# Linear attention and a SiLU layer on one core: moving batch 1's softmax steps, W2's first rows and batch 3's loads

## The chip, the core and the metric

The kernel runs on one core of a Trainium2 chip. The core has TensorE (PE, matrix products into PSUM), VectorE (DVE), ScalarE (ACT), GpSimd (POOL) and SyncE (SP), each with its own queue of instructions that it works through in order, and 16 DMA engines that all of them share. The time is that of the device for one execution, in microseconds (us); the figure of a kernel is the median of its runs.

## What is computed

Eight batches, eight heads, 576 positions, 64 columns a head. Attention without the square matrix: q is softmaxed over its 64 columns, k over the positions, and both meet through a 64 x 64 matrix. The result, 4608 rows of 512, goes through a layer with a SiLU.

```python
q_s = softmax(q, axis=-1); k_s = softmax(k, axis=2)
kv  = einsum('bhsd,bhse->bhde', k_s, v)
x   = einsum('bhsd,bhde->bhse', q_s, kv)   # -> x: (4608, 512)
h   = x @ w_in                             # w_in: (512, 2048)
out = (h * sigmoid(h)) @ w_out             # w_out: (2048, 512)
```

Inputs and output are float32; the products run in fp16 and bf16.

## The kernel before

The work is cut into nine chunks of 512 rows of x (`TCH`); the attention is done by batch (576 rows), so that chunk t needs batches up to t. Chunk 0 is special: its first layer is done over all 576 rows of batch 0 (`wide`, 16 blocks of 128 columns of w_in, line 258), so the first 64 columns of chunk 1 (counted along the rows of x) are already there and are copied from GTS[0] to GTS[1]. From chunk 1 on, the two layers are done in the form of Strassen and Winograd: seven products instead of eight, with sums and differences of blocks made on VectorE ahead of them. Their names are WS (`ws_op`, differences of w_in, line 319), XS (`xs_op`, of x, line 329), S (`s_op`, of the SiLU's result GT, line 442) and T (`t_op`, of W2, line 452; T3 is written over a quarter of W2). `group` (line 368) does products of the first layer, `prod` (line 468) of the second; `mm2_plain` (line 405) is chunk 0's second layer, one block of W2's rows at a time, `mm1` (line 276) half of chunk 1's first. `group_snap` copies a group's partial sums from PSUM to a tile h, `group_add` (line 346) adds another to it.

The attention of a batch b has these steps. `load` brings q, k and v in halves `cc` (four heads each) into two buffers per name. `exp_q` (line 108) makes eq; its sums over the 64 columns come from VectorE alone (`qsum`, lines 148 and 150), or, for batch 1, from `qsum_pair` and `qsum_end`: GpSimd adds the halves of the 64 columns twice (lines 126 and 129), and VectorE reduces the 16 that are left (line 136) and inverts them. `qnorm` (line 157) multiplies eq in place. Then eq is transposed, by TensorE (`tr`, line 175, with `trcopy` out of PSUM) for batches 0 and 1 and by a DMA (`q_transpose`, line 167) later. `exp_k` (line 113) makes ek, `vcast` (line 91 or 89) puts v into vaug as bf16, `kv` (line 189) multiplies them, `kvcopy` (lines 200 and 202) divides, and `xt` (line 228) makes the columns of x for a chunk in tiles XT.

The order is written out by hand. `units` is a list of pieces of TensorE's work, and `plan(u, f)` puts f ahead of unit u; `begin[t]` (b1 for chunk 1) is the unit at which a chunk starts. In the order in which this list is walked, each engine gets its instructions, and each works them off in that order. Units 0 to 15 are the blocks of `wide`; from b1 come nine units of `mm2_plain`, then `mm2_plain` and `group` in turn, then eight of `mm1`; `full(t)` lays out chunks 2 to 6. Within a unit the plans are taken in the order in which they stand.

```python
for u, f in enumerate(units):
    for g in at.get(u, ()):
        g()
    f()
```

Loads come from two queues. Before chunk 1 is done they are issued by GpSimd (w_in, w_out with a change of type from float32 to fp16, and q, k, v of batches 1 and 2), later by SyncE, which also stores the output. The tiles of W2 are loaded four blocks of rows at a time (`load_w2`). A load waits for its buffer's last reader; in SyncE's queue everything behind it waits with it.

Of the kernel before, what the change touches and what calls it, by code (L numbers as in the profile page):

```python
# [17 lines left out]
def kernel(  # L18
# [9 lines left out]
    nc = tc.nc  # L28
    B, H, S, D = q.shape
# [3 lines left out]
    J = S // P  # L33
# [4 lines left out]
    TCH = 512  # L38
# [23 lines left out]
    GTS = [glob.tile([128, NFB, S], FP16, name="GT0"), glob.tile([128, NFB, TCH], FP16, name="GT1")]  # L62
# [24 lines left out]
    def copy(eng, o, i):  # L87
        if eng is nc.scalar:
            eng.copy(out=o, in_=i)  # L89
        else:  # L90
            eng.tensor_copy(o, i)  # L91

    def load(b, name, src, cc, eng):
        t = ld.tile([128, 2, J * D], FP32, name=name)
        st[b][name, cc] = t
        x = src[b].rearrange("(g r) (p j) d -> g (r p) (j d)", r=2, j=J)
        eng.dma_start(out=t, in_=x.rearrange("g x y -> x g y")[:, 2 * cc:2 * cc + 2, :])

    def jgd(b, name, cc):
        return st[b][name, cc].rearrange("p g (j d) -> p j g d", d=D)  # L100

    def half(t, cc):
        return t[:, :, cc * 128:(cc + 1) * 128].rearrange("p j (g d) -> p j g d", d=D)

    def exp_q(b, cc, g0=0, g1=2):
        if "eq" not in st[b]:
            st[b]["eq"] = ap.tile([128, J, NG * D], BF16, name="eq")
        nc.scalar.activation(  # L108
            out=half(st[b]["eq"], cc)[:, :, g0:g1], in_=jgd(b, "qt", cc)[:, :, g0:g1], func=ACT.Exp
        )  # L110

    def exp_k(b, cc):
        nc.scalar.activation(out=half(ek, cc), in_=jgd(b, "kt", cc), func=ACT.Exp)  # L113
# [6 lines left out]
    def qsum_pair(b, cc):  # L120
        e = half(st[b]["eq"], cc)
        t1 = mp.tile([128, 2 * TCH], FP32, name="h0", bufs=1)[:, 0:J * D]
        t1 = t1.rearrange("p (j g d) -> p j g d", g=2, d=D // 2)
        t2 = mp.tile([128, 2 * TCH], FP32, name=f"h{cc + 1}", bufs=1)[:, 0:J * D // 2]
        t2 = t2.rearrange("p (j g d) -> p j g d", g=2, d=D // 4)
        nc.gpsimd.tensor_tensor(
            out=t1, in0=e[:, :, :, 0:D // 2], in1=e[:, :, :, D // 2:D], op=ALU.add
        )
        nc.gpsimd.tensor_tensor(
            out=t2, in0=t1[:, :, :, 0:D // 4], in1=t1[:, :, :, D // 4:D // 2], op=ALU.add  # L130
        )
        st[b]["t2", cc] = t2

    def qsum_end(b, cc):
        new_zq(b)
        nc.vector.reduce_sum(out=st[b]["zq"][:, cc], in_=st[b]["t2", cc], axis=AX.X)
        nc.vector.reciprocal(out=st[b]["rzq"][:, cc], in_=st[b]["zq"][:, cc])

    def new_zq(b):
        if "zq" not in st[b]:  # L140
            st[b]["zq"] = ap.tile([128, 2, J, 2], FP32, name="zq", bufs=2)
            st[b]["rzq"] = ap.tile([128, 2, J, 2], FP32, name="rzq", bufs=2)
# [11 lines left out]
    def qnorm(b, cc, eng):  # L154
        e = half(st[b]["eq"], cc)
        r = st[b]["rzq"][:, cc]
        eng.tensor_tensor(  # L157
            out=e, in0=e, in1=r[:, :, :, None].to_broadcast([128, J, 2, D]), op=ALU.mult
        )

    def new_qt(b):
        if "qT" not in st[b]:
            st[b]["qT"] = ap.tile([128, J, 2, 128], BF16, name="qT", bufs=2)
        return st[b]["qT"]
# [7 lines left out]
    def tr(b, cc, j0, j1, bank):  # L172
        t = PS[:, bank, :].bitcast(BF16)
        for j in range(j0, j1):
            nc.tensor.transpose(
                out=t[:, (j - j0) * 128:(j - j0 + 1) * 128],
                in_=st[b]["eq"][:, j, cc * 128:(cc + 1) * 128],
                identity=ident,
            )

    def trcopy(b, cc, j0, j1, bank, eng=nc.vector):
        t = PS[:, bank, :].bitcast(BF16)[:, 0:(j1 - j0) * 128].rearrange("x (j y) -> x j y", y=128)
        copy(eng, new_qt(b)[:, j0:j1, cc, :], t)
# [25 lines left out]
    def kv_both(b):  # L209
        kv(b, 0)  # L210
        kv(b, 1)
        kvcopy(b)
# [25 lines left out]
    def xt(t, cc, eng=nc.scalar):  # L238
        got = pieces(t)
        for b, col, n, dst in got:  # L240
            xt_mm(b, cc, col, n, 6, dst)
        xt_evac(t, cc, 6, got[0][3], TCH, got[0][3], eng)
# [62 lines left out]
    def wa(c, f):  # L305
        return W1[:, 2 * c:2 * c + 2, f * 128:(f + 4) * 128]
# [4 lines left out]
    def ws_op(i, g):  # L311
        w, f0, f1 = WS[g], 4 * g + 8, 4 * g
        in0, in1, op = {
            1: (wa(0, f1), wa(1, f1), ALU.add),
            2: (w[0], wa(0, f0), ALU.subtract),
            3: (wa(0, f0), wa(0, f1), ALU.subtract),
            4: (wa(1, f0), w[1], ALU.subtract),
        }[i]
        nc.vector.tensor_tensor(out=w[i - 1], in0=in0, in1=in1, op=op)
# [30 lines left out]
    def group_silu(t, i, f, n):  # L350
        x = group_bank(t, False) if i is None else four(t, i)
        nc.scalar.activation(out=group_out(t, f, n), in_=x, func=ACT.Silu, scale=1.0 / XS)  # L352
# [46 lines left out]
    def store(t, col, o):  # L399
        for i in range(2):  # L400
            nc.sync.dma_start(out=rows(t, col + i * P), in_=o[i * P:(i + 1) * P, :])
# [11 lines left out]
    def mm2_plain_out(t, m, eng):  # L413
        if m % 2 == 0:
            st[t]["ow"] = mp.tile([128, 2, DM], FP32, name="ow", bufs=3)
        o = st[t]["ow"][:, m % 2]
        if eng is nc.scalar:
            nc.scalar.activation(out=o, in_=PS[:, 2 + m], func=ACT.Copy, scale=OS)
        else:
            nc.vector.tensor_scalar_mul(out=o, in0=PS[:, 2 + m], scalar1=OS)  # L420
        store(t, m * 128, o)
# [22 lines left out]
    def t_op(i, eng, f0=0, f1=HF):  # L444
        o, in0, in1 = {
            1: (T1, B12, B11),
            2: (T2, B22, T1),
            3: (T3, B22, B12),
            4: (T4, B21, T2),
        }[i]  # L450
        f = slice(f0, f1)
        eng.tensor_tensor(out=o[:, f], in0=in0[:, f], in1=in1[:, f], op=ALU.subtract)  # L452
# [97 lines left out]
    def load_w2(f0, f1):  # L550
        nc.gpsimd.dma_start(
            out=W2[:, f0:f1, :],
            in_=w_out[f0 * 128:f1 * 128, :].rearrange("(fc p) o -> p fc o", p=128),
        )
# [10 lines left out]
    load_w1(8, 16, 2, 4)  # L565
    load(1, "qt", q, 0, nc.gpsimd)
    load(1, "qt", q, 1, nc.gpsimd)
    load(1, "kt", k, 0, nc.gpsimd)
    load(1, "kt", k, 1, nc.gpsimd)
    load_w2(0, 4)  # L570
    load_w2(4, 8)
    load(1, "vt", v, 0, nc.gpsimd)
    load(1, "vt", v, 1, nc.gpsimd)
# [39 lines left out]
    def plan(u, f):  # L613
        at.setdefault(u, []).append(f)
# [141 lines left out]
    for i in (1, 2, 6, 5, 7, 4, 3):  # L756
# [3 lines left out]

    b1 = begin[1]

    plan(9, lambda: (load_w2(8, 12), exp_q(1, 0), qsum_pair(1, 0)))
    plan(12, lambda: (exp_q(1, 1, 0, 1), qsum_end(1, 0), qnorm(1, 0, nc.gpsimd)))
    plan(12, lambda: load(2, "qt", q, 0, nc.gpsimd))
    plan(13, lambda: (exp_q(1, 1, 1, 2), qsum_pair(1, 1)))
    plan(14, lambda: load(2, "qt", q, 1, nc.gpsimd))
    plan(b1 + 2, lambda: (exp_k(1, 0), exp_k(1, 1)))
    plan(b1 + 1, lambda: (tr(1, 0, 0, 5, 6), tr(1, 0, 5, J, 7)))
    plan(b1 + 1, lambda: (trcopy(1, 0, 0, 5, 6, nc.scalar), trcopy(1, 0, 5, J, 7)))  # L770
    plan(b1, lambda: (qsum_end(1, 1), qnorm(1, 1, nc.vector)))
    plan(b1, lambda: load_w2(12, 16))
    plan(b1, lambda: nc.gpsimd.tensor_copy(GTS[1][:, :, 0:64], GTS[0][:, :, TCH:S]))
    plan(b1 + 3, lambda: (load(2, "kt", k, 0, nc.gpsimd), load(2, "kt", k, 1, nc.gpsimd)))
    plan(b1 + 6, lambda: (load(2, "vt", v, 0, nc.gpsimd), load(2, "vt", v, 1, nc.gpsimd)))
    plan(b1 + 4, lambda: vcast(1, 0, nc.scalar))
# [17 lines left out]
    plan(b1 + 17, lambda: (vcast(2, 0, nc.gpsimd), vcast(2, 1, nc.gpsimd)))  # L794
    plan(b1 + 22, lambda: (group_silu(1, 2, 4, 1), group_silu(1, 0, 12, 0)))
    plan(b1 + 18, lambda: t_op(1, nc.vector))
    plan(b1 + 23, lambda: mm2_plain_out(0, 0, nc.scalar))
    plan(b1 + 23, lambda: (load(3, "qt", q, 0, nc.sync), load(3, "kt", k, 1, nc.sync)))
    plan(b1 + 23, lambda: mm2_plain_out(0, 1, nc.vector))
    plan(b1 + 24, lambda: group_silu(1, 1, 12, 1))  # L800
    plan(b1 + 24, lambda: (ws_op(1, 0), ws_op(2, 0)))
    plan(b1 + 24, lambda: [load(3, x, y, i, nc.sync) for x, y, i in (
        ("vt", v, 0), ("vt", v, 1), ("kt", k, 0), ("qt", q, 1)
    )])
    plan(b1 + 25, lambda: kv_both(2))
    plan(b1 + 26, lambda: t_op(2, nc.vector))
    plan(b1 + 27, lambda: xt(2, 0, nc.vector))
    plan(b1 + 28, lambda: t_op(4, nc.vector))
    plan(b1 + 29, lambda: xt(2, 1))
# [40 lines left out]
```

The softmax here doesn't subtract the row's maximum and nothing guards it: scores larger than these inputs give would overflow.

## Time and profile before

| | us |
|---|---|
| median of 5 runs | 264.38 (264.09 to 264.59) |
| the profiled execution | 264.04 |
| its span | 262.3 |
| TensorE busy | 252.5 |
| VectorE busy | 208.4 |
| ScalarE busy | 186.6 |
| GpSimd busy | 67.8 |

The span is the part of the execution from the first instruction to the last; the rest lies around it. In a timeline each row is one group of equal instructions in a row: start, time, engine, line, operation, output<-input, shapes, count, and in brackets how long the engine stood idle before it and what released it. L405 is line 405 of the kernel. Ends of matrix products are modelled, so holes in TensorE are better counted from start to start.

### The profile page before, as it was taken

What the parts mean: (1) busy time and instruction counts of PE and PEld (TensorE: products, weight loads), DVE (VectorE), ACT (ScalarE), POOL (GpSimd) and SP (SyncE); (2) the same over time, 40 slices, a digit from 0 to 9 for tenths busy, and PEclk for the clock granted to TensorE, in tenths of its full rate; (3) what the DMA queues carried; (4) which work ended last, traced back from release to release, by engine and by line L of the source; (5) the groups of instructions that cost most, each with busy time, mean ns of one, the idle gap of its engine ahead of it and who ended that gap; (6) DMA issues with size and microseconds to landing.
All of it is one profiled execution on the core that took longest, in us unless ns stands there. A gap on an engine that the chain in (4) does not pass through costs nothing.

```text
span 262.3 us, 6406 instructions
## 1 busy us (share of the span) xinstructions
PE 252.5 (96%) x2732; PEld 203.0 (77%) x2732; DVE 208.4 (79%) x268; ACT 186.6 (71%) x210; POOL 67.8 (26%) x63
## 2 busy tenths in 40 slices
PE   8799999999899999999999999999999999999993
PEld 3457655656788888888888888888888888888882
DVE  2867777799997999799979997999798448855932
ACT  4766874898796699669966997699664757584610
POOL 1653792550450306030603060306000000000004
PEclk9999999999999999999999999999999999999998
DMA  7999999669987487858874889650425002500534
GB/s 246 339 185 324 266 317 331 264 124 308 399 325 165 149 205 276 133 183 202 279 180 139 200 281 119 198 118 2 90 51 112 2 0 48 115 2 1 117 85 120
DMA packets 35452, 45.89 MB, mean 175 GB/s; under 512 B 16208, under 2 KB 19984, under 8 KB 35424
## 3 DMA queue, kind: packets, MB, share of 16 engines
q1 hardware_dynamic: 29488, 33.63, 47.0%
q0 software_dynamic: 5616, 11.60, 17.1%
q8 instruction: 21, 0.34, 0.5%
q10 hardware_dynamic: 320, 0.26, 0.4%
q14 instruction: 7, 0.06, 0.1%
HBM read 36.70 MB, written 9.44 MB: 176 GB/s over the span
## 4 chain that ended last, share of the span: by engine, by line
PE 74%; DVE 9%; DMA 9%; issue 4%; ACT 2%; POOL 1%; POOLq 0%; DVEq 0%; ACTq 0%
PE PS L468 33%; PE PS L368 31%; DMA W<-in_moe_w_out_dram 6%; PE PS L405 4%; DMA W<-in_moe_w_in_dram 3%; PE PS L228 2%; PE PS L189 2%; DVE h L346 2%; DVE S L442 1%; DVE zq L148 1%; DVE T L452 1%; DVE GT L442 1%; ACT ek L113 1%; POOL out_dram L730 1%; PE PS L276 1%
## 5 line engine op out<-in xcount | busy, mean ns | idle before, releaser
L346 DVE TENSOR_TENSOR h<-PS,h 128x1024 f32<-128x1024 f32 (+1 forms) x45 | 54.0, 1199 | 12.0 <-PE PS L368 6.0
L468 PEld LDWEIGHTS <-GT 128*128 128x128 f16 x512 | 49.5, 98 | 6.9 <-issue 1.0
L368 PEld LDWEIGHTS <-WS 128*128 128x128 f16 x480 | 46.7, 98 | 7.1 <-issue 1.0
L468 PE MATMUL PS<-W,GT 128*128 128x256 f16 x384 | 49.1, 273 | 0.0
L368 PE MATMUL PS<-XS,WS 128*128 128x256 f16 (+1 forms) x360 | 46.3, 272 | 0.2
L352 ACT ACTIVATE GT<-h 128x1024 f16<-128x1024 f32 (+1 forms) x45 | 46.1, 1047 | 0.3 <-DVE h L346 0.3
L89 ACT COPY h<-PS 128x1024 f32<-128x1024 f32 (+1 forms) x35 | 35.1, 1003 | 13.2 <-PE PS L368 12.5
L157 POOL TENSOR_TENSOR eq<-eq,rzq 128x1152 bf16<-128x1152 bf16 x13 | 27.5, 2117 | 56.7 <-DVE rzq L152 52.7
L468 PEld LDWEIGHTS <-S 128*128 128x128 f16 x384 | 37.0, 98 | 6.3 <-DVE S L442 1.0
L368 PEld LDWEIGHTS <-W 128*128 128x128 f16 x360 | 34.6, 98 | 4.8 <-issue 0.5
L468 PE MATMUL PS<-T,S 128*128 128x256 f16 x256 | 32.7, 273 | 0.8 <-DVE S L442 0.8
L368 PE MATMUL PS<-XT,W 128*128 128x256 f16 (+1 forms) x240 | 29.5, 272 | 0.1
L352 ACT ACTIVATE GT<-PS 128x1024 f16<-128x1024 f32 (+1 forms) x15 | 15.2, 1016 | 18.9 <-PE PS L368 18.9
L91 POOL CAST vaug<-vt 128x1152 bf16<-128x1152 f32 x12 | 15.4, 1289 | 45.9 <-DMA vt<-in_v_dram 37.5
L730 POOL DMA_DIRECT2D out_dram<-ow x5 | 2.7, 545 | 72.1 <-DVE ow L715 72.1
L108 ACT ACTIVATE eq<-qt 128x1152 bf16<-128x1152 f32 (+1 forms) x17 | 18.8, 1108 | 2.6 <-DMA qt<-in_q_dram 2.6
L113 ACT ACTIVATE ek<-kt 128x1152 bf16<-128x1152 f32 x16 | 18.4, 1155 | 2.8 <-DMA kt<-in_k_dram 2.8
L148 DVE TENSOR_REDUCE zq<-eq 128x18 f32<-128x1152 bf16 x12 | 16.1, 1345 | 3.9 <-ACT eq L108 3.9
L258 PE MATMUL PS<-XT,W 128*128 128x288 f16 x128 | 16.3, 286 | 0.5 <-DVE XT L91 0.2
L468 PE MATMUL PS<-W,S 128*128 128x256 f16 x128 | 16.5, 273 | 0.0
L488 DVE SCALAR_TENSOR_TENSOR ow<-PS,sc 128x512 f32<-128x512 f32 x7 | 4.8, 692 | 14.4 <-ACT sc L484 14.4
L405 PE MATMUL PS<-W,GT 128*128 128x512 f16 x64 | 15.6, 380 | 0.2 <-DMA W<-in_moe_w_out_dram 0.2
(78 smaller groups left out, 344.4 us busy)
## 6 DMA issues: line engine op xcount, KB each, us to landing
out_dram<-ow SPq DMA_DIRECT2D x64, 128.0 KB, 2.4
qt<-in_q_dram SPq DMA_DIRECT2D x12, 576.0 KB, 4.7
kt<-in_k_dram SPq DMA_DIRECT2D x12, 576.0 KB, 5.9
vt<-in_v_dram SPq DMA_DIRECT2D x12, 576.0 KB, 5.4
qt<-in_q_dram POOLq DMA_DIRECT2D x4, 576.0 KB, 11.3
kt<-in_k_dram POOLq DMA_DIRECT2D x4, 576.0 KB, 12.1
vt<-in_v_dram POOLq DMA_DIRECT2D x4, 576.0 KB, 12.0
W<-in_moe_w_out_dram POOLq DMA_DIRECT2D x4, 512.0 KB, 15.1
```

Source lines behind the costliest of these rows:

```text
L89: eng.copy(out=o, in_=i)
L91: eng.tensor_copy(o, i)
L108: nc.scalar.activation(out=half(st[b]["eq"], cc)[:, :, g0:g1], in_=jgd(b, "qt", cc)[:, :, g0:g1], func=ACT.Exp)
L113: nc.scalar.activation(out=half(ek, cc), in_=jgd(b, "kt", cc), func=ACT.Exp)
L148: nc.vector.reduce_sum(out=z, in_=e, axis=AX.X)
L157: eng.tensor_tensor(out=e, in0=e, in1=r[:, :, :, None].to_broadcast([128, J, 2, D]), op=ALU.mult)
L258: nc.tensor.matmul(out=PS[:, 2 * (fb % 3) + n, 0:S // 2], lhsT=W1[:, c, fb * 128:(fb + 1) * 128], rhs=XTS[0][:, c, n * (S // 2):(n + 1) * ...
L346: nc.vector.tensor_tensor(out=four(t, i), in0=group_bank(t, True), in1=four(t, i), op=ALU.add)
L352: nc.scalar.activation(out=group_out(t, f, n), in_=x, func=ACT.Silu, scale=1.0 / XS)
L368: nc.tensor.matmul(out=PS[:, bank + p // 2, (p % 2) * HT:(p % 2) * HT + width(t)], lhsT=a[:, c, p * 128:(p + 1) * 128], rhs=bb[:, c, 0:wid ...
L405: nc.tensor.matmul(out=PS[:, 2 + tb, :], lhsT=GTS[t % 2][:, fc, tb * 128:(tb + 1) * 128], rhs=W2[:, fc, :], start=(fc == 0), stop=(fc == N ...
L468: nc.tensor.matmul(out=PS[:, bank, m * HN:(m + 1) * HN], lhsT=a[:, fc, m * 128:(m + 1) * 128], rhs=bb[:, fc, :], start=(first and fc == 0) ...
```

## The change

Seven moves, all in the order and none in the arithmetic. Batch 1's first exp of q is made in two halves, one ahead of block 9 and one ahead of block 10 of `wide`. The GpSimd sums of both halves of the heads now stand ahead of the GpSimd norm of the first, and the loads of batch 2's q behind it. Batch 1's first transposes and their copies stand two units later, behind its exps of k. The copy of chunk 1's first 64 columns goes from GpSimd to ScalarE and eight units later. W2's first four blocks of rows are loaded ahead of batch 1's k. Batch 3's six loads stand together in SyncE's queue ahead of chunk 0's eight stores, in the order q, k, k, v, v, q (before: q, k, then stores, then v, v, k, q, then stores). WS1 of group 0 is made eleven units earlier, and T2 two.

```diff
     load(1, "qt", q, 1, nc.gpsimd)
+    load_w2(0, 4)
     load(1, "kt", k, 0, nc.gpsimd)
     load(1, "kt", k, 1, nc.gpsimd)
-    load_w2(0, 4)
     load_w2(4, 8)
...
-    plan(9, lambda: (load_w2(8, 12), exp_q(1, 0), qsum_pair(1, 0)))
-    plan(12, lambda: (exp_q(1, 1, 0, 1), qsum_end(1, 0), qnorm(1, 0, nc.gpsimd)))
-    plan(12, lambda: load(2, "qt", q, 0, nc.gpsimd))
-    plan(13, lambda: (exp_q(1, 1, 1, 2), qsum_pair(1, 1)))
-    plan(14, lambda: load(2, "qt", q, 1, nc.gpsimd))
+    plan(9, lambda: (load_w2(8, 12), exp_q(1, 0, 0, 1)))
+    plan(10, lambda: (exp_q(1, 0, 1, 2), qsum_pair(1, 0)))
+    plan(12, lambda: (exp_q(1, 1, 0, 1), qsum_end(1, 0)))
+    plan(13, lambda: (exp_q(1, 1, 1, 2), qsum_pair(1, 1), qnorm(1, 0, nc.gpsimd)))
+    plan(14, lambda: (load(2, "qt", q, 0, nc.gpsimd), load(2, "qt", q, 1, nc.gpsimd)))
     plan(b1 + 2, lambda: (exp_k(1, 0), exp_k(1, 1)))
-    plan(b1 + 1, lambda: (tr(1, 0, 0, 5, 6), tr(1, 0, 5, J, 7)))
-    plan(b1 + 1, lambda: (trcopy(1, 0, 0, 5, 6, nc.scalar), trcopy(1, 0, 5, J, 7)))
+    plan(b1 + 3, lambda: (tr(1, 0, 0, 5, 6), tr(1, 0, 5, J, 7)))
+    plan(b1 + 3, lambda: (trcopy(1, 0, 0, 5, 6, nc.scalar), trcopy(1, 0, 5, J, 7)))
     plan(b1, lambda: (qsum_end(1, 1), qnorm(1, 1, nc.vector)))
     plan(b1, lambda: load_w2(12, 16))
-    plan(b1, lambda: nc.gpsimd.tensor_copy(GTS[1][:, :, 0:64], GTS[0][:, :, TCH:S]))
+    plan(b1 + 8, lambda: nc.scalar.copy(out=GTS[1][:, :, 0:64], in_=GTS[0][:, :, TCH:S]))
...
+    plan(b1 + 23, lambda: [load(3, x, y, i, nc.sync) for x, y, i in (
+        ("qt", q, 0), ("kt", k, 1), ("kt", k, 0), ("vt", v, 0), ("vt", v, 1), ("qt", q, 1)
+    )])
     plan(b1 + 23, lambda: mm2_plain_out(0, 0, nc.scalar))
-    plan(b1 + 23, lambda: (load(3, "qt", q, 0, nc.sync), load(3, "kt", k, 1, nc.sync)))
     plan(b1 + 23, lambda: mm2_plain_out(0, 1, nc.vector))
     plan(b1 + 24, lambda: group_silu(1, 1, 12, 1))
-    plan(b1 + 24, lambda: (ws_op(1, 0), ws_op(2, 0)))
-    plan(b1 + 24, lambda: [load(3, x, y, i, nc.sync) for x, y, i in (
-        ("vt", v, 0), ("vt", v, 1), ("kt", k, 0), ("qt", q, 1)
-    )])
+    plan(b1 + 13, lambda: ws_op(1, 0))
+    plan(b1 + 24, lambda: ws_op(2, 0))
     plan(b1 + 25, lambda: kv_both(2))
-    plan(b1 + 26, lambda: t_op(2, nc.vector))
+    plan(b1 + 24, lambda: t_op(2, nc.vector))
     plan(b1 + 27, lambda: xt(2, 0, nc.vector))
```

## The prediction, made before the result was known

> **What bounds the kernel now.** First the page: is one engine full, and at full clock?
>
> ```profile
> span 262.3 us, 6406 instructions
> PE 252.5 (96%) x2732; PEld 203.0 (77%) x2732; DVE 208.4 (79%) x268; ACT 186.6 (71%) x210; POOL 67.8 (26%) x63
> PE   8799999999899999999999999999999999999993
> PEclk9999999999999999999999999999999999999998
> ```
>
> TensorE is, so time can only come from its gaps. Then stages, in the windows view:
>
> ```profile
> 15.56:32.36 16.80, 16.30 (x128) 12.38 (x129) 11.91 (x18) 12.13 (x20) 8.23 (x10) 1.00 1.13 276
> 32.36:45.00 12.64, 12.20 (x147) 6.55 (x148) 9.16 (x18) 7.90 (x10) 8.75 (x10) 1.00 1.14 313
> 56.00:72.03 16.03, 15.14 (x189) 10.33 (x188) 15.54 (x22) 13.39 (x20) 3.18 (x3) 1.00 0.97 317
> 84.00:244.00 160.00, 159.96 (x1762) 138.41 (x1760) 133.45 (x156) 119.10 (x127) 26.21 (x16) 1.00 0.51 129
> ```
>
> Columns: length, then busy PE, PEld, DVE, ACT, POOL, clock, DMA share, GB/s. From 84 to 244 nothing is to be had. From 56 to 72 VectorE is busy 15.54 of 16.03. The gaps are in TensorE's timeline:
>
> ```profile
> 28.05 4.08 PE L258 MATMUL PS<-XT,W 128*128 128x288 f16 x32 [0.21 <-DVE GT L251]
> 32.36 1.04 PE L405 MATMUL PS<-W,GT 128*128 128x512 f16 x4 [0.23 <-DMA W<-in_moe_w_out_dram]
> ...
> 33.74 3.62 PE L405 MATMUL PS<-W,GT 128*128 128x512 f16 x16
> 37.63 0.66 PE L175 MATMUL PS<-ident,eq 128*128 128x128 bf16 x9 [0.27 <-ACT vaug L89]
> ...
> 70.22 1.04 PE L468 MATMUL PS<-W,GT 128*128 128x256 f16 x8
> 72.03 1.05 PE L468 MATMUL PS<-T,S 128*128 128x256 f16 x8 [0.77 <-DVE S L442]
> ```
>
> Counted start to start, with steady steps of 0.98 (eight of 288 columns), 0.86 (four of 512) and 0.87 (eight of 256), the holes are 0.38 before 28.05, 0.39 before 32.36, 33.74 + 4 x 0.86 = 37.18 against 37.63: 0.45, and 70.22 + 0.87 = 71.09 against 72.03: 0.94. Two more of 0.29 stand at 67.61 and 81.91, each behind an addition of line 346 on VectorE. The chain of waits is nearly all VectorE from 58.5 to 81.9. At 37.63 the label says ScalarE's v cast, but what the transpose needs is the norm on VectorE (35.95 + 1.53 = 37.48).
>
> **A row and a rule for the second half.** VectorE, then GpSimd:
>
> ```profile
> 52.32 1.85 DVE L452 TENSOR_TENSOR T<-W 128x2048 f16<-128x2048 f16 x1
> ...
> 69.99 1.99 DVE L442 TENSOR_TENSOR S<-S,GT 128x2048 f16<-128x2048 f16 x1
> ...
> 77.77 2.34 DVE L442 TENSOR_TENSOR GT<-GT 128x2048 f16<-128x2048 f16 x1
> ...
> 81.78 1.21 DVE L442 TENSOR_TENSOR S<-GT,S 128x2048 f16<-128x2048 f16 x1
> ```
>
> ```profile
> 50.98 2.12 POOL L157 TENSOR_TENSOR eq<-eq,rzq 128x1152 bf16<-128x1152 bf16 x1 [0.42 <-DVE rzq L152]
> ...
> 67.65 1.16 POOL L91 CAST vaug<-vt 128x1152 bf16<-128x1152 f32 x1 [11.37 <-DMA vt<-in_v_dram]
> 69.18 1.73 POOL L91 CAST vaug<-vt 128x1152 bf16<-128x1152 f32 x1 [0.36 <-DMA vt<-in_v_dram]
> ...
> 76.91 2.12 POOL L157 TENSOR_TENSOR eq<-eq,rzq 128x1152 bf16<-128x1152 bf16 x1 [1.11 <-DVE rzq L152]
> ```
>
> The fp16 operation of 2048 takes 1.21 alone and 1.99 or 2.34 under a GpSimd operation; the cast takes 1.16 alone and 1.73 when it meets one. The ends fit a lock: the operation of 77.77 ends 1.08 after the norm's end at 79.03, the one of 69.99 ends 1.07 after the cast's at 70.91. The Trainium skill, "SBUF — State Buffer", section "SBUF: two separate sides", calls the shared port pair an exclusive lock that the first holds for its whole instruction. It speaks against this change, which brings batch 3's casts forward. Read as shared bandwidth, the slow cast would cost VectorE 0.57 wherever it falls, and bringing it forward changes nothing: 0.64 in all below. Read as a lock, a cast costs nothing behind an operation that doesn't use the pair (the cast of 67.65 beside the copy from PSUM), and a full 1.0 ahead of one that does. I take the lock.
>
> **The change, part by part.**
>
> Exps in halves. 0.68 twice for 1.17 once, on ScalarE, with a tanh (0.65, step 0.57) between. Half a starts at 25.50, the tanh of block 9 (counted from 0) at 26.08 instead of 26.57, its product on VectorE ends 27.51; block 12, which takes its bank, may start at 27.67, on time: 0.38 gone. But half b ends at 27.32 (before: 26.67), GpSimd's two sums (1.28 and 0.80) end at 29.57, and VectorE's reduction (line 136, 29.24 before) waits until 29.60. Queued behind it is the product of block 12, 30.27 to 31.02, which frees block 15's bank: that last block starts at 31.07 instead of 30.98. So the 0.38 is given back whole.
>
> W2's first rows. They pass two k loads in GpSimd's queue. The loads come in one after the other (2.4 for 512 KB of weights, 1.5 for a k), so the rows land at 29.4, not 32.3, and k at 30.9 and 32.3. The exps of k can't start before 32.8: hidden by 0.5 and 1.6; beyond that it would be paid one for one in front of ScalarE's copies. The first product starts when the last block ends: 32.05. Gain 0.31.
>
> Sums ahead of the norm. GpSimd: sums of the second half 30.34 to 32.51, then the norm until 34.65. VectorE reduces after its last product (33.6), norms 34.4 to 36.0. The first transposes, now two units later, are reached at 32.05 + 3 x 0.86 = 34.63 and start at about 34.75: a new wait of 0.12. The second are reached at 36.97, with the norm done at 36.0: 0.45 gone. Net in front: 0.31 + 0.45 - 0.12 = 0.64. Bounds: 0.3 (if the chain of sums slips by 0.35 more) to 0.8.
>
> Queue moves on GpSimd. The loads of q for batch 2 issue at 34.6 and 35.4 (before 32.19 and 35.07), W2's last rows at 36.1 (35.79). The stream of transfers is full until 40.3, so none lands later. With the copy of 1.83 gone, k and v of batch 2 issue 1.5 sooner, into the same stream: nothing.
>
> The copy on ScalarE. Nearest row: ScalarE's copies of 1024 elements, 1.01; it stands in the 3.04 of idle time before 42.18. Bounds 0.7 and 1.8 (GpSimd's row): both covered. Without the cover, 1.0 in front of XT. On the other side it frees VectorE's WS (1.19, of which 0.5 was the lock), which nothing waits for.
>
> WS and T2 earlier. WS (0.7) goes into VectorE's idle 0.85 before 49.12. T2 (1.21) ahead of batch 2's kv: it ends at 57.2, kv at 57.0, the copies of kvn at 57.9; their reader comes at 58.5. Cost nothing; but a gain neither, since VectorE's next, the XT copy, waits for that reader's product, 59.59 - 0.64 = 58.95, with VectorE idle before it.
>
> Batch 3's loads. All six go ahead of eight stores. The transpose issue ends at 55.25; six issues of 0.6 follow. The stores slip by about 2 and land near 69.5; the first that needs their buffer is the addition at 84.48. Before, the v casts came at 67.65 and 69.18, in front of S: 0.07 + 0.77 = 0.8 of VectorE's chain. When do they come now? The load after a transpose lands 4.4 after its issue (81.89, cast at 86.43), the next ones 1.5 apart (casts at 113.08 and 114.56): q 59.7, k 61.2 and 62.7, v 64.2 and 65.7; with a second load as slow as k's after 95.31 (2.0 to 2.8) up to 65.5 and 67.0. The page "DMA: Bandwidth & Descriptors" of the Trainium skill, section "Anatomy of one DMA — SWDGE (gpsimd) path", fits 2.0 + bytes/436e3, for loads from the other queue: an estimate of 3.35, then 1.35 each, so v at 62.7. By that figure both casts fall on the XS operations and the sum turns to +0.6. I take the rows.
>
> VectorE then, shifted by 0.64: XS 63.0 to 64.6, T3 64.55 to 65.8 (all users of the pair), the addition and copy from PSUM until 68.0, S 68.0 to 70.5. If v lands after 64.55, the first cast waits for T3 and runs to 66.8, the second to 67.8, both beside PSUM work: no cost, and the 0.8 is gained. TensorE: the wait at 72.03 shrinks from 0.94 to about 0.13; the holes at 67.61 and 81.91 stay, as both sides move alike. ScalarE's wait for k (1.4 before 70.53) goes too, but VectorE was later still.
>
> Sum: 0.64 + 0.8 = 1.45 of the profiled 264.04 (span 262.3); that execution was 0.34 under the median of 264.38, so the forecast is 264.38 - 1.45 = 262.9.
>
> **The rivals.** (B) One cast gets in ahead of T3: v lands between 64.1 and 64.55 and a waiting GpSimd beats VectorE's next operation, as the waiting T operation of 52.32 beat the next cast. T3 and all after it 1.0 later: -1.45 + 1.0 = -0.45, 263.9. A v so late that the second cast meets S costs up to 0.8, much the same. For it: the landing is near this border. Against: any slow second load.
>
> (C) Slower: v lands before 64.1. The first cast takes the pair among XS, the second (1.5 later, 65.6 at most) takes it again before T3. 2 x 1.03 of lock on the chain that ends in S: -1.45 + 2.05 = +0.6, 265.0. For it: the page's figure, and the early stores gone from between the loads. Against: 4.4 measured for the first.
>
> (E) The front gains nothing: sums and norm on GpSimd slip and the transposes wait for all that was won. Then only S: 263.6.
>
> **The numbers.** About 0.2% (0.53) is what a measurement of this kernel can tell. Forecast 0.45 (its own range 262.5 to 263.4), B 0.20, C 0.22, E 0.13. Faster: nearly all of the forecast, 0.4 of B, 0.65 of E: 0.60. Slower: C and a little: 0.23. Same: 0.17. The range goes from 262.5 to 264.9, into C, leaving out under 2 in 10.
>
> **What would show it.** Right: the L405 products start near 32.05 with no wait on W; no hole before the second L175 group, a small one before the first; a late L136; both vaug casts of batch 3 between 64 and 68 with 1.16 each; S at 1.2 twice; a short wait before T,S. Wrong: XS or W of line 452 at twice their time beside a cast (B, C); a hole at the first L175 of 0.5 or more (E); a wait at the XT copies for ScalarE.

## The result, and the profile after

| | before | after |
|---|---|---|
| median, us | 264.26 (263.8 to 265.06, 37 runs) | 263.37 (262.41 to 264.32, 19 runs) |
| ratio | | 0.9961, 95% interval 0.9952 to 0.997 |
| the profiled execution | 264.04 | 263.61 |

Faster by 0.4%, some 0.9 us; the forecast was 262.9, 1.45 under a median of 264.38 that is 264.26 with all runs of before. The runs of after lie apart in a way that those of before don't: five at 262.41 to 262.76, thirteen at 263.1 to 263.68, one at 264.32. The granted clock is 0.996 to 1.0 in all of them, so it is not what parts them.

The page and the windows of after, with the same stages as before, shifted as the products that bound them (the last is again 160 us of the full stage):

```profile
span 261.8 us, 6412 instructions
PE 252.9 (97%) x2732; PEld 203.3 (78%) x2732; DVE 208.1 (79%) x268; ACT 187.7 (72%) x212; POOL 65.7 (25%) x62
```

```profile
15.49:31.87 16.38, 16.13 (x129) 12.50 (x129) 11.85 (x18) 11.88 (x20) 7.57 (x10) 1.00 1.13 280
31.87:44.09 12.22, 12.05 (x150) 6.46 (x147) 8.68 (x18) 9.15 (x11) 7.68 (x9) 1.00 1.14 309
55.10:71.17 16.07, 15.00 (x189) 10.31 (x187) 14.89 (x21) 13.64 (x20) 2.64 (x3) 1.00 0.98 319
83.05:243.05 160.00, 160.00 (x1764) 138.69 (x1762) 132.94 (x155) 118.78 (x126) 26.20 (x16) 1.00 0.51 129
```

The first two stages are shorter by 0.42 each. The third is no shorter (16.07 for 16.03), although VectorE has 0.65 less to do in it. TensorE's timeline of after says where the holes are (rows left out are marked with dots):

```profile
30.89 1.14 PE L258 MATMUL PS<-XT,W 128*128 128x288 f16 x8 [0.19 <-DVE GT L251]
31.87 2.75 PE L405 MATMUL PS<-W,GT 128*128 128x512 f16 x12
34.57 0.68 PE L175 MATMUL PS<-ident,eq 128*128 128x128 bf16 x9
35.08 1.89 PE L405 MATMUL PS<-W,GT 128*128 128x512 f16 x8
36.81 0.67 PE L175 MATMUL PS<-ident,eq 128*128 128x128 bf16 x9
...
65.54 1.04 PE L468 MATMUL PS<-W,GT 128*128 128x256 f16 x8
67.65 1.03 PE L368 MATMUL PS<-XS,WS 128*128 128x256 f16 x8 [1.07 <-DVE h L346]
...
70.27 1.04 PE L468 MATMUL PS<-W,GT 128*128 128x256 f16 x8
71.17 1.05 PE L468 MATMUL PS<-T,S 128*128 128x256 f16 x8
...
79.96 1.04 PE L468 MATMUL PS<-W,GT 128*128 128x256 f16 x8
81.47 1.03 PE L368 MATMUL PS<-XS,WS 128*128 128x256 f16 x8 [0.48 <-DVE h L346]
```

The same place of the third stage in before, beside the row of 67.65:

```profile
66.45 1.04 PE L468 MATMUL PS<-W,GT 128*128 128x256 f16 x8
67.61 1.03 PE L368 MATMUL PS<-XS,WS 128*128 128x256 f16 x8
```

Start to start, as before: the hole of 0.38 ahead of block 12 is gone, one of 0.36 has come ahead of block 15 (30.89). L405 starts without a wait for W (31.87), the first transposes 0.12 after their turn (34.57 against 31.87 + 3 x 0.86 = 34.45), the second on time. At 67.65 the hole is 1.24 (65.54 + 0.87 = 66.41) where it was 0.29, at 71.17 it is nearly nothing where it was 0.94, at 81.47 it is 0.65 where it was 0.29. VectorE, then GpSimd, show what stands behind the last three (after):

```profile
63.62 0.42 DVE L329 TENSOR_TENSOR XS<-XT 128x512 f16<-128x512 f16 x1
63.95 1.37 DVE L329 TENSOR_TENSOR XS<-XT,XS 128x512 f16<-128x512 f16 x1
65.25 1.21 DVE L452 TENSOR_TENSOR W<-W 128x2048 f16<-128x2048 f16 x1
...
69.89 1.22 DVE L442 TENSOR_TENSOR S<-S,GT 128x2048 f16<-128x2048 f16 x1
...
75.72 0.27 DVE L152 RECIPROCAL rzq<-zq 128x18 f32<-128x18 f32 x1
...
76.98 2.70 DVE L442 TENSOR_TENSOR GT<-GT 128x2048 f16<-128x2048 f16 x1
```

```profile
63.86 1.20 POOL L91 CAST vaug<-vt 128x1152 bf16<-128x1152 f32 x1 [8.48 <-DMA vt<-in_v_dram]
66.85 1.16 POOL L91 CAST vaug<-vt 128x1152 bf16<-128x1152 f32 x1 [1.79 <-DMA vt<-in_v_dram]
...
76.47 2.12 POOL L157 TENSOR_TENSOR eq<-eq,rzq 128x1152 bf16<-128x1152 bf16 x1 [1.47 <-ACT GT L352]
```

And VectorE in before, where the last XS, T3 and the reciprocal ahead of the norm stand so:

```profile
64.86 0.42 DVE L329 TENSOR_TENSOR XS<-XT,XS 128x512 f16<-128x512 f16 x1
65.20 1.22 DVE L452 TENSOR_TENSOR W<-W 128x2048 f16<-128x2048 f16 x1
...
76.51 0.27 DVE L152 RECIPROCAL rzq<-zq 128x18 f32<-128x18 f32 x1
```

S is free of the casts (1.22, before 1.99). But the first cast of batch 3 starts at 63.86, during the third XS, and the fourth XS, which VectorE comes to right behind it, takes 1.37 instead of 0.42: it ends 0.26 after the cast. T3 and all behind it are 0.95 late. Lower down, S over GT (76.98) takes 2.70 instead of 2.34, because GpSimd's norm starts at 76.47, 0.48 after the reciprocal that it needs had ended (75.99); before it was 0.13 (76.78 to 76.91). In the chain of waits the first of these stalls has no releaser; it stands as "issue", 1.23 long where the chain of before has 0.27:

```profile
63.28 0.74 DVE XS L329 x2
64.02 1.23 issue
65.25 1.21 DVE W L452
```

Sum against the profile of before, in us gained: `wide` starts 0.07 earlier; front 0.75 (0.38 - 0.36 + 0.40 - 0.12 + 0.45); batch 1's kv 0.09 (39.87 - 39.13 = 0.74, before 40.78 - 39.95 = 0.83); S 0.91 (0.94 - 0.03); first cast -0.95; norm -0.35; a new hole ahead of 73.88 -0.08. Together 0.44; the executions differ by 264.04 - 263.61 = 0.43.

### The profile page after: what moved, and what is told of

The parts are those of the page before. It is cut to its first block, busy times and chain, and to the rows that moved or that the text cites. A ratio compares the mean times of both kernels' runs of the same rounds, so it can differ in the third digit from the quotient of the medians.

```text
span 261.8 us, 6412 instructions
## 1 busy us (share of the span) xinstructions
PE 252.9 (97%) x2732; PEld 203.3 (78%) x2732; DVE 208.1 (79%) x268; ACT 187.7 (72%) x212; POOL 65.7 (25%) x62
## 4 chain that ended last, share of the span: by engine, by line
PE 79%; DVE 9%; DMA 4%; ACT 2%; POOL 2%; issue 1%; SPq 1%; POOLq 0%; DVEq 0%; ACTq 0%
PE PS L468 33%; PE PS L368 31%; PE PS L405 5%; DMA vt<-in_v_dram 4%; PE PS L258 3%; PE PS L228 2%; PE PS L189 2%; DVE h L346 2%; PE PS L276 1%; DVE GT L442 1%; DVE zq L148 1%; DVE S L442 1%; SPq L97 1%; POOL out_dram L730 1%; ACT sg L250 1%
## 5 line engine op out<-in xcount | busy, mean ns | idle before, releaser
L368 PEld LDWEIGHTS <-W 128*128 128x128 f16 x360 | 34.7, 98 | 4.8 <-issue 0.5
L258 PEld LDWEIGHTS <-W 128*128 128x128 f16 x128 | 12.4, 98 | 4.3 <-issue 1.3
```

The costliest lines, as they stand in the source:

```text
L258: nc.tensor.matmul(out=PS[:, 2 * (fb % 3) + n, 0:S // 2], lhsT=W1[:, c, fb * 128:(fb + 1) * 128], rhs=XTS[0][:, c, n * (S // 2):(n + 1) * ...
L368: nc.tensor.matmul(out=PS[:, bank + p // 2, (p % 2) * HT:(p % 2) * HT + width(t)], lhsT=a[:, c, p * 128:(p + 1) * 128], rhs=bb[:, c, 0:wid ...
```

## The experiments

Every kernel was timed in five rounds, beside a run of before on the same chip (its median: 263.92 in the first group, 264.26 in the second, 264.14 in the third). Edits are against after, but for the second; lines between the pieces of an edit are marked with dots.

**The two halves apart.** First: batch 3's loads at their old places, the rest changed.

```diff
-    plan(b1 + 23, lambda: [load(3, x, y, i, nc.sync) for x, y, i in (
-        ("qt", q, 0), ("kt", k, 1), ("kt", k, 0), ("vt", v, 0), ("vt", v, 1), ("qt", q, 1)
-    )])
     plan(b1 + 23, lambda: mm2_plain_out(0, 0, nc.scalar))
+    plan(b1 + 23, lambda: (load(3, "qt", q, 0, nc.sync), load(3, "kt", k, 1, nc.sync)))
...
+    plan(b1 + 24, lambda: [load(3, x, y, i, nc.sync) for x, y, i in (
+        ("vt", v, 0), ("vt", v, 1), ("kt", k, 0), ("qt", q, 1)
+    )])
```

> The changed kernel with batch 3's six loads back at their old places among the stores; all else of the change stays. If the front is worth 0.64 to 0.9 by itself (the first products 0.4 earlier, the hole before the second transposes gone) and the casts meet S again as before, this runs at 263.4 to 263.6, and its runs lie close together. If all of the gain came from the loads, it runs as before (264.3). VectorE's S at twice 1.3 to 2.0 again and a hole of about 0.9 before the T,S products.

Measured: 263.66, ratio 0.9987 (0.9976 to 0.9998). Its profile (263.74) has the front of after, the old hole ahead of T,S (1.02), no long XS, and the late norm with S over GT at 2.70. The medians differ by 0.26 where 0.64 to 0.9 was expected: the late norm, unknown when that was written, takes back 0.35, and the hole ahead of T,S is 0.08 longer. Second: before, with nothing but the six loads together. The edit is the same diff read the other way.

> The kernel before with only batch 3's six loads moved together ahead of the stores. v then lands near 64.6 while VectorE is at XS (63.7 to 65.2) and T3 (65.2 to 66.4), the same phase as in the changed kernel. If a cast takes the port pair ahead of an XS or T operation, 1.0 is paid there and 0.8 won at S: 264.3 to 264.5, no gain; a run in which it waits behind T3 would be 0.8 faster. If the casts only share bandwidth, or the loads themselves were the gain, 263.5 in all runs.

Measured: 263.59, ratio 0.9991 (0.9978 to 1.0005), runs from 263.01 to 264.52. Neither half alone is told from no change by much; what each does is read in its trace. In this one T3 came first, and the cast had to wait:

```profile
65.18 1.22 DVE L452 TENSOR_TENSOR W<-W 128x2048 f16<-128x2048 f16 x1
```

```profile
65.19 2.23 POOL L91 CAST vaug<-vt 128x1152 bf16<-128x1152 f32 x1 [8.92 <-DMA vt<-in_v_dram]
```

T3 has its normal 1.22 and the cast takes 2.23, which costs VectorE nothing. T3 started 0.01 sooner, and so had the pair (the port pair that VectorE and GpSimd share). It is not the 0.8 that was expected of such a run, since v's second half lands late (67.75) and its cast meets S: S takes 1.56, and 0.45 of the hole ahead of T,S stays. So a late landing costs too, at S; in the profile with the reduction one unit later (below), where S takes 1.96, it is 0.79.

**Is it the cast ahead of T3?** One tiny GpSimd copy that reads the last XS (a gate), put ahead of T3, makes everything behind it in GpSimd's queue, the cast first, wait until the last XS is done. The loads stay where they are.

```diff
-    plan(begin[2] + 1, lambda: t_op(3, nc.vector))
+    plan(begin[2] + 1, lambda: (nc.gpsimd.tensor_copy(gate, XS4[3][0:1, 0, 0:1]), t_op(3, nc.vector)))
```

> The changed kernel with a 1 x 1 copy on GpSimd that reads the last XS tile, ahead of batch 3's casts: they can't start before T3 has the pair. Lock: the last XS at 0.42 instead of 1.37, the casts beside the addition and the copy from PSUM, the hole at 67.65 back to 0.3, and all runs in the lower cluster: 262.4 to 262.7, 0.9 under the changed kernel's median, with a small spread. Rival (the hole is the addition's own lateness, or the cast's cost is the same wherever it falls): 263.4, as the changed kernel.

Measured: 262.53, ratio 0.9947 (0.9932 to 0.9962), faster than before; four of six runs within 262.37 to 262.57. The other two are at 263.06 and 263.14, and the profile is of the last of these. Its XS (0.42), T3 (1.22) and norm are as expected; what it has more stands in `wide`:

```profile
17.20 14.46 PE L258 MATMUL PS<-XT,W 128*128 128x288 f16 x112 [0.48 <-DMA W<-in_moe_w_in_dram]
```

A block of `wide` waits for its rows of w_in, and L405 starts at 32.83 instead of 31.87. Such a wait stands in two more profiles (WS and T2 back 0.30, reduction later 0.32) and in neither of the two of after. So it, too, spreads runs by some tenths, whatever the casts do.

The kernel was run again in the third group:

> The kernel with the one gate on GpSimd again, as the neighbour of the last one on the same chip. As before: no cast during the last XS, XS 0.42 and T3 1.22, the norm of batch 3 starting 0.11 after its wait, and 0.9 under the changed kernel: 262.5. If the first series was a lucky one, it comes at the changed kernel's 263.4.

Measured: 262.44 (262.4 to 262.58), ratio 0.993 (0.9918 to 0.9942). This profile can be laid beside that of after: its L405 starts at 31.86, its kv at 39.13, as there. Then, VectorE, GpSimd and TensorE:

```profile
63.96 0.42 DVE L329 TENSOR_TENSOR XS<-XT,XS 128x512 f16<-128x512 f16 x1
64.29 1.22 DVE L452 TENSOR_TENSOR W<-W 128x2048 f16<-128x2048 f16 x1
...
76.19 2.35 DVE L442 TENSOR_TENSOR GT<-GT 128x2048 f16<-128x2048 f16 x1
```

```profile
64.44 1.11 POOL L813 CAST gate<-XS 1x1 f32<-1x1 f16 x1 [9.06 <-DVE XS L329]
65.50 1.15 POOL L91 CAST vaug<-vt 128x1152 bf16<-128x1152 f32 x1
66.84 1.16 POOL L91 CAST vaug<-vt 128x1152 bf16<-128x1152 f32 x1 [0.19 <-DMA vt<-in_v_dram]
```

```profile
66.70 1.03 PE L368 MATMUL PS<-XS,WS 128*128 128x256 f16 x8
...
80.34 1.03 PE L368 MATMUL PS<-XS,WS 128*128 128x256 f16 x8
```

T3 starts at 64.29 instead of 65.25. The tiny copy comes 0.15 after T3 and so stands behind it itself (it takes 1.11), and the cast comes behind the copy; the product of 67.65 comes at 66.70, that of 81.47 at 80.34. Of these 1.13, 0.95 is the cast, 0.35 the norm, which is on time here, and 0.17 is given back ahead of T,S (70.39), where the second cast meets S (67.69, 1.38). The execution is 1.17 shorter.

**After again, and the others, as to who came first.** After was run in the second group as a neighbour:

> The changed kernel as it is, beside the others on the same chip: 263.4, in clusters near 262.6 and 263.5 if one cast ahead of T3 or behind it makes the difference; one broad heap if not.

Measured: 263.43, ratio 0.9964 (0.9949 to 0.998), one run at 262.33 and eight at 263.05 to 263.79. Its cast started at 64.28, during the last XS; T3, next at 64.42, took 2.17. With this, eight profiles show the same race:

| kernel | cast starts | VectorE's operation at that border | takes | cast takes |
|---|---|---|---|---|
| after | 63.86 | XS, 63.95 | 1.37 | 1.20 |
| after again | 64.28 | T3, 64.42 | 2.17 | 1.24 |
| GpSimd pad (below) | 64.27 | T3, 64.42 | 2.17 | 1.25 |
| exp in one piece (below) | 64.59 | T3, 64.65 | 2.18 | 1.18 |
| W2 late (below) | 64.84 | T3, 64.88 | 2.19 | 1.16 |
| only the loads | 65.19 | T3, 65.18 | 1.22 | 2.23 |
| WS and T2 back (below) | 64.93 | T3, 64.80 | 1.22 | 2.11 |
| reduction later (below) | 65.17 | T3, 64.79 | 1.22 | 1.86 |

Whoever starts first has the pair; the closest two are 0.04 apart (W2 late, the cast first) and 0.01 (only the loads, T3 first). The loser does its own work only then: T3 of after again ends at 66.59, 1.07 behind the cast's end at 65.52.

**Both casts ahead of T3.** The two v loads first of the six, and a gate behind the first XS, so that both casts stand waiting among the XS operations, as in rival C.

```diff
-        ("qt", q, 0), ("kt", k, 1), ("kt", k, 0), ("vt", v, 0), ("vt", v, 1), ("qt", q, 1)
+        ("vt", v, 0), ("vt", v, 1), ("qt", q, 0), ("kt", k, 1), ("kt", k, 0), ("qt", q, 1)
...
-        plan(u, lambda: (xs_op(t, 1), xs_op(t, 2), xs_op(t, 3), xs_op(t, 4)))
+        plan(u, lambda: (
+            xs_op(t, 1), t == 2 and nc.gpsimd.tensor_copy(gate, XS4[0][0:1, 0, 0:1]),
+            xs_op(t, 2), xs_op(t, 3), xs_op(t, 4),
+        ))
```

> The changed kernel with batch 3's v as the first of the six loads, and a 1 x 1 copy on GpSimd that reads the first XS tile, ahead of the casts: both casts then wait while XS runs, the first takes the pair ahead of the last XS, the second ahead of T3. Lock in order of arrival: twice 1.0 on VectorE's chain, an XS of 1.4 and a T3 of 2.2, a hole of about 2.3 at 67.7: 1.0 over the changed kernel, 1.9 over the kernel with the casts behind T3 (264.3 to 264.6). If VectorE keeps the pair over operations that follow each other: 262.6. The late q and k could add ScalarE's waits near 66.

Measured: 264.73, ratio 1.0021 (1.0004 to 1.0037), six runs at 264.0 to 264.23 and six at 265.23 to 265.59. The profile is of the lower group; VectorE, GpSimd, TensorE:

```profile
63.38 1.38 DVE L329 TENSOR_TENSOR XS<-XT 128x512 f16<-128x512 f16 x1
64.68 1.37 DVE L329 TENSOR_TENSOR XS<-XT,XS 128x512 f16<-128x512 f16 x1
65.97 1.21 DVE L452 TENSOR_TENSOR W<-W 128x2048 f16<-128x2048 f16 x1
```

```profile
63.12 2.65 POOL L91 CAST vaug<-vt 128x1152 bf16<-128x1152 f32 x2
```

```profile
68.37 1.03 PE L368 MATMUL PS<-XS,WS 128*128 128x256 f16 x8 [2.04 <-DVE h L346]
```

Each cast costs the XS behind it 0.95, and the hole is 2.20: 0.29 and twice 0.95. It was the third and the fourth XS, where the fourth and T3 had been expected; the price is the same. The two engines take turns, cast, XS, cast, XS: VectorE, with work at hand all the time, does not get two in a row here while a GpSimd operation waits. What the upper group has more was not seen in a profile and stays open; five of its six runs have a granted clock of 0.993 or 0.994, the lower group 0.998 or more, but the sixth has 1.0.

**The late norm.** In after GpSimd has 62 busy rows on the page, in before 63: the copy that went to ScalarE. Either the norm waits for something else, or its start hangs on where it stands in GpSimd's stream. So one tiny operation is added to that stream, some 35 us ahead of the norm.

```diff
+    plan(b1 + 10, lambda: nc.gpsimd.memset(gate, 0.0))
```

> The changed kernel with one more instruction for GpSimd, a 1 x 1 memset in its idle time near 41. In the profiles so far, GpSimd's norm of batch 3's second half starts 0.44 after its wait has ended in the kernels that lost the copy, and 0.11 in those with one instruction more. If this hangs on the place in GpSimd's stream of instructions, the norm starts after 0.11 here, VectorE's S over GT takes 2.35 instead of 2.70, the hole at 81.5 shrinks from 0.65 to 0.30, and the time falls by 0.35 (263.0 to 263.1). If it comes from what the other engines or the transfers do at that time, all stays: 263.4.

Measured: 262.96, ratio 0.9949 (0.9931 to 0.9967), beside 263.43 (0.9949 to 0.998) for after: the intervals overlap, so it is the trace that decides. VectorE, then GpSimd:

```profile
75.85 0.27 DVE L152 RECIPROCAL rzq<-zq 128x18 f32<-128x18 f32 x1
...
77.11 2.35 DVE L442 TENSOR_TENSOR GT<-GT 128x2048 f16<-128x2048 f16 x1
```

```profile
76.25 2.12 POOL L157 TENSOR_TENSOR eq<-eq,rzq 128x1152 bf16<-128x1152 bf16 x1 [1.11 <-DVE rzq L152]
```

The norm starts 0.13 after the reciprocal's end (76.12) and S over GT is back at 2.35; the race ahead of T3 is lost as before (2.17). It holds for every profile of this study: with 62 rows (after, after again, and five of the experiments) the norm is late and S over GT takes 2.69 or 2.70; with 63 (before, only the loads, both runs of the gated kernel, the pad, both casts ahead, the last one below) it takes 2.34 or 2.35. The bracket of the late norm in after names ScalarE's GT, but it names the reciprocal in the profile of the front alone, as late, and GT in that of the last kernel, on time. So the place in the stream decides; what happens there was not shown.

**WS and T2 at their old places.**

```diff
-    plan(b1 + 13, lambda: ws_op(1, 0))
-    plan(b1 + 24, lambda: ws_op(2, 0))
+    plan(b1 + 24, lambda: (ws_op(1, 0), ws_op(2, 0)))
...
-    plan(b1 + 24, lambda: t_op(2, nc.vector))
+    plan(b1 + 26, lambda: t_op(2, nc.vector))
```

> The changed kernel with WS1 of group 0 and T2 at their old places. By the prediction these two moves neither cost nor gain, since the XT copy waits for TensorE anyway: 263.4, with the same two clusters. If they carry part of the gain, 0.6 (one WS) to 1.2 (T2) slower.

Measured: 262.91, ratio 0.996 (0.9945 to 0.9974), not slower than after. T3 won the race in its profile, and `wide` lost some 0.6 by waits that the moves don't touch (w_in among them). The moves themselves bring nothing that can be told from the scatter.

**Exp in one piece.**

```diff
-    plan(9, lambda: (load_w2(8, 12), exp_q(1, 0, 0, 1)))
-    plan(10, lambda: (exp_q(1, 0, 1, 2), qsum_pair(1, 0)))
+    plan(9, lambda: (load_w2(8, 12), exp_q(1, 0), qsum_pair(1, 0)))
```

> The changed kernel with batch 1's first exp in one piece at unit 9 again and its sums behind it. By the prediction the halves give back at block 15 what they save at block 12: a hole of 0.38 before block 12, none before block 15, the first L405 product at the same time within 0.1, and the time within 0.1 of the changed kernel: 263.4. If the halves carry a gain of their own: 0.4 slower, 263.8.

Measured: 263.52, ratio 0.9971 (0.9958 to 0.9984), against 0.9964 for after beside it. The hole of 0.61 ahead of block 12 is back, that of block 15 is gone, another of 0.28 comes among the L405 products. L405 starts 0.14 and kv 0.36 later than in after (32.01 and 39.49), but q, for which the exp waits, lands 0.17 later too (25.52 for 25.35). The medians, 263.52 and 263.43, tell no gain of the halves from the scatter; 0.2 is not excluded.

**What else the front holds.** First W2's rows behind k again:

```diff
-    load_w2(0, 4)
     load(1, "kt", k, 0, nc.gpsimd)
     load(1, "kt", k, 1, nc.gpsimd)
+    load_w2(0, 4)
```

> W2's first four blocks of rows are loaded behind batch 1's k again, the rest is as in the changed kernel. If the early rows are what gave the front its gain, the first L405 product waits for W2 again: it starts at 32.3 instead of 31.87, with a hole of 0.4 in front of it; the first transposes (31.87 + 3 x 0.86 = 34.45 before, 34.57 with their wait of 0.12) then come at 34.9 with no wait of their own, and the kv of batch 1 at 39.4 instead of 39.13. All after it is later by 0.3: 263.7 against the 263.4 of the changed kernel. If another wait (the sums on GpSimd and the norm behind them) sets the transposes anyway, kv stays at 39.1 and the time at 263.4.

Measured: 263.64, ratio 0.998 (0.9966 to 0.9994). TensorE:

```profile
31.20 1.14 PE L258 MATMUL PS<-XT,W 128*128 128x288 f16 x8 [0.20 <-DVE GT L251]
32.57 2.76 PE L405 MATMUL PS<-W,GT 128*128 128x512 f16 x12 [0.23 <-DMA W<-in_moe_w_out_dram]
35.17 0.67 PE L175 MATMUL PS<-ident,eq 128*128 128x128 bf16 x9
```

The wait for W is back (31.20 + 0.98 = 32.18, and 32.57 - 32.18 = 0.39), the wait at the transposes is gone: from block 15 to the transposes 3.97 instead of 3.68 in after, so 0.29 lost, as expected (block 15 itself is 0.31 later than in after, by small holes in `wide`). Then the reduction of the first sums one unit later:

```diff
-    plan(12, lambda: (exp_q(1, 1, 0, 1), qsum_end(1, 0)))
-    plan(13, lambda: (exp_q(1, 1, 1, 2), qsum_pair(1, 1), qnorm(1, 0, nc.gpsimd)))
+    plan(12, lambda: exp_q(1, 1, 0, 1))
+    plan(13, lambda: (qsum_end(1, 0), exp_q(1, 1, 1, 2), qsum_pair(1, 1), qnorm(1, 0, nc.gpsimd)))
```

> VectorE's reduction of batch 1's first sums (L136) goes one unit later, behind the product that it held up. My account: the hole of 0.36 ahead of block 15 goes, L405 starts at 31.5, but VectorE then comes to the reduction 0.7 later, GpSimd's norm starts as before behind its second sums (30.3 to 32.4), ends at 34.5, and the first transposes, reached at 34.1, wait for it 0.4: the hole has only moved, and the time is that of the changed kernel within 0.1 (263.3 to 263.5). The other: the hole at block 15 is real time, and it is won whole: 263.05.

Measured: 263.19, ratio 0.9962 (0.9948 to 0.9975), like after. Block 15 starts on time, but 0.28 opens among the L405 products (32.89), which now wait for GT of the last blocks. The last kernel has this edit and the gate, and the first transposes and their copies one unit later (`b1 + 4` for `b1 + 3`).

> Three edits on the changed kernel: the gate that keeps batch 3's first v cast behind T3, the reduction one unit later, and the first transposes one unit later (four of the nine L405 units ahead of them instead of three), so that they don't meet the end of GpSimd's norm. If the holes ahead of block 15 (0.36) and of the first transposes (0.12) were all that is left in front, kv of batch 1 starts at 38.7 instead of 39.13, and the time is 0.4 under the gated kernel beside it: 262.1. If the kv then waits for batch 1's v cast (landed at about 38 in the changed kernel, cast after it), only 0.1 is won: 262.4.

Measured: 262.52 (262.25 to 263.48), ratio 0.9938 (0.9921 to 0.9955), the same as the gated kernel beside it (0.9918 to 0.9942). TensorE:

```profile
31.65 3.84 PE L405 MATMUL PS<-W,GT 128*128 128x512 f16 x16
35.33 0.67 PE L175 MATMUL PS<-ident,eq 128*128 128x128 bf16 x9
...
39.01 0.81 PE L189 MATMUL PS<-vaug,ek 64*64 64x65 bf16 x72
```

kv comes 0.12 sooner than in after (39.13). The expectation of 0.4 fell, and not by the v cast that its other case named: kv did not wait. Holes of 0.16 ahead of L405 and of 0.23 within it took the place of those removed. What is left in front is, as these holes are read here, the pace at which ScalarE and VectorE finish GT; no run tests that.

The best versions are the gated kernel (262.53 and 262.44) and this one (262.52). The first needs one small GpSimd copy on top of the change.

## Why the prediction was right, and where not

The side was right, the range held the time, and the number was 0.5 low. In part that is luck. The profiled execution is 0.43 shorter, which looks like the 0.45 of rival B; but front and S won more than worked out, and the norm's loss, which no case had, took it back.

- **Front, 0.64 forecast, 0.84 measured.** The second transposes' 0.45 and the new wait of 0.12 came as worked out, and the wait for W2's rows went whole: 0.40, where 0.31 was counted because block 15 was to start 0.09 later than before; it lost only 0.36, against the 0.38 won at block 12. The exps in halves bring nothing that could be told, as said. The 0.09 of kv had not been counted: in before VectorE's v cast ran until 40.31, into kv (39.95), in after until 38.74.
- **S, 0.8 forecast, 0.91 measured.** The casts no longer meet S; the hole ahead of T,S closed.
- **The lock, taken against shared bandwidth, is what the traces show.** The Trainium skill, "SBUF — State Buffer", section "SBUF: two separate sides", says exclusive and for the whole instruction: 0.95 for each cast that came first, nothing on VectorE for each that came second.
- **The step that failed: that v lands after 64.55, so that the first cast waits for T3.** Its own rows had said 64.2, and v's first half landed at 63.71 and 64.14 in the two profiles of after: the first load of the six took 3.96 and 4.15 where 4.4 was counted, and no slow one stood in front of v, on which the forecast had counted. VectorE, 0.26 further ahead than worked out, would have come to T3 at 64.29 already. The page "DMA: Bandwidth & Descriptors", section "Anatomy of one DMA — SWDGE (gpsimd) path", would have had it at 62.7 by the estimate made from it; no profile with these loads in this order shows it before 63.71. What came was rival B, at the price named for it: 1.0 forecast, 0.95 measured. Its border was wrong: at 63.71 the text had both casts in front of T3, but the second v landed 3.0 after the first (66.70), not 1.5, and its cast cost nothing. The likeliest case was put on the wrong side of a border that its own estimate already stood on.
- **Not foreseen: the norm's late start, 0.35.** The copy's move to ScalarE was costed at nothing for GpSimd, and by its work it was; by shifting GpSimd's stream by one it cost 0.35, which the pad takes back in its trace.
- **WS, T2 and the copy: nothing**, as forecast. The copy takes 1.05 in ScalarE's idle time (39.15).
- **The size.** With the cast kept behind T3 the forecast's sum can be read whole: 264.04 - 262.44 = 1.60 between profiled executions, where 1.45 was worked out. The median of after lies between this and the 0.45 of rival B. That its runs at 262.41 to 262.76 are those in which T3 wins is likely: 263.61 - 0.95 = 262.66. It is not shown, since no profile of after fell among them, and the waits for w_in spread runs as well.

## What to carry to other kernels

When a change moves a GpSimd operation next to VectorE operations that use the shared pair, work out not only how much they overlap but which starts first, and where a load decides that by a few tenths, hold GpSimd back with a small dependent operation rather than trust the landing. Here the stall had no releaser in the chain of waits; it was found by an operation of 0.42 that took 1.37. An estimate that falls on a border should be priced on both sides of it, and not only on the good one.

## What the runs showed of the hardware

VectorE's next operation, queued and ready, does not keep the pair against a waiting GpSimd: with both casts ahead, casts and XS took turns, and the XS took 1.38 and 1.37 instead of 0.42. And GpSimd can start 0.48 instead of 0.13 after what it waits for, at one place of its stream, and no more (0.13) once one tiny operation is added ahead of it. The Trainium skill, "Runtime: NRT & Kernel Launch", section "Instruction fetch mechanics", tells of instructions that are fetched in blocks, with the crossing mostly hidden; whether this is such a place no run here shows.
